# The experts' second product with tokens instead of features on PSUM's partitions

## The chip, the core and the metric

One core of a Trainium2 chip runs the program. The metric is device time in microseconds (us) of one execution. Engines are named as in the profile: PE is TensorE, PEld its weight loads, DVE is VectorE, ACT is ScalarE, POOL is GpSimd, SP is the queue that issues the DMAs.

## What is computed

Linear attention on 4 batches of 576 rows, then four experts whose outputs are added with a weight per token, then a gated dense layer. Only the experts are touched by the change:

```python
def _moe_ref(x, domain_probs, w1, w2):          # x: 2304 tokens x 512
    p = domain_probs / (domain_probs.sum(-1, keepdims=True) + 1e-09)
    out = np.zeros((N, D), dtype=np.float32)
    for e in range(E):                          # 4 experts, 1024 hidden features each
        h = np.maximum(x @ w1[e], 0.0)
        out += p[:, e:e + 1] * (h @ w2[e])
    return out
...
    x = _moe_ref(x=x, **moe_kwargs)
    return _moe2_ref(x=x, **moe2_kwargs)        # (silu(x @ wg) * (x @ wv)) @ wo, 1536 hidden
```

## The kernel before

The 2304 tokens are worked on in two halves of 1152. A half has two blocks of columns: X has 512 tokens, Y has 640. Hidden features are cut into units of 256: 16 expert units (kind "e", 4 per expert) and 6 gated units (kind "g") in each half, 44 units in all, numbered 0 to 43; a step is one unit on one block, so a half has 32 expert steps and 12 gated ones. Every large float32 product is three passes of float32r: an operand is split into a high part (a cast on ACT, `split`, line 98) and the rest (a subtraction on DVE or POOL, line 99).

In a step, `stage_h` makes the hidden features by seven products of half-sized operands (Winograd's form of Strassen's, `chain`). Each product is six matmuls on PE, of 256 columns for X and 320 for Y; their sums lie in three PSUM banks. ACT copies the first bank away after products 1, 6, 7 and 4 (`sn`, line 482, and line 500), and DVE adds (lines 488, 497, 503) to get four quadrants of `g`. In an expert step DVE then applies the ReLU and the token's weight in one instruction on each half of the tokens (`expert`, line 623), ACT casts the high part `hh` (line 628), and DVE makes the low part `hl` at the start of the next step (line 632). The weights lie on all 128 partitions in the order of the columns (`pbc`), brought there by broadcasting DMAs.

`stage_y` is the second product. In the step after, in chunks between the seven products, it multiplies `hh` and `hl` by the unit's second weights (`oh`, `ol`). In an expert step the weights are the stationary operand and the tokens move: a tile is 128 model features by 256 or 320 tokens, six matmuls long, and there are eight of them; DVE adds each to `acc` (line 701), which is kept transposed, features on partitions. In a gated step the tokens are stationary: a tile is 128 tokens by 512 features, and there are four (X) or five (Y); DVE adds with line 716.

`WEAVE` says after which of the step's products how many chunks of the step before run. PE and ACT execute from step 2 on in the order of the program; DVE and POOL in the order that a scheduler gives them when the kernel is built. Where an operand is not ready, the engine waits and so does all that stands behind it on that engine. PSUM's eight banks are held by tags with a number of buffers: `hA` and `hB` two each, `hC`, `at` one each, `y` two.

At the turn from experts to gated units (unit 15 to 16, and 37 to 38), the sums in `acc` become the next layer's tokens. `combine_x` makes seven operands of them, in two stages for each pair of model tiles (j = 0, 1): casts on ACT (`xh`), low parts on DVE and POOL (`xl`), four subtractions on DVE in place (lines 396 to 399), then more casts and low parts. Steps count from 0: in a half of 44 steps, ML = 32 is the step of the first gated unit on X, and `AX_`, `AY_` say at which product of ML-1 and ML each stage is issued.

While the first half's experts run, other work shares the engines: the attention of batches 2 and 3, and the decoding of the gated layers' float64 weights, 36 pieces with five DVE instructions each (lines 538 to 545). In the second half nothing of that is left.

## Time and profile before

| | |
|---|---|
| device time, median of 3 executions | 1384.72 us (1378.69 to 1385.62) |
| the profiled execution: span from first to last instruction | 1383.4 us |
| PE busy | 1289.2 us, 93% of the span |
| DVE busy | 1141.1 us, 82% |
| ACT busy, POOL busy | 595.6 us (43%), 569.7 us (41%) |
| mean granted TensorE clock | 0.976 of full |
| from the first product of unit 2 on X to that of unit 15 on Y (first half's experts) | 131.4 to 511.3 us |
| units 24 to 36 (second half's experts) | 821.5 to 1128.9 us |

The span of the profiled execution lies inside the range of the three times. Busy shares over the whole span are means over stages with different limits, so the stages are read one by one. PE's busy time overlaps itself, because matmuls are pipelined: the time that a matmul takes from the next one is the distance of their starts.

### The profile page before, as it was taken

What the parts mean: (1) busy time and instruction counts of PE and PEld (TensorE: products, weight loads), DVE (VectorE), ACT (ScalarE), POOL (GpSimd) and SP (SyncE); (2) the same over time, 40 slices, a digit from 0 to 9 for tenths busy, and PEclk for the clock granted to TensorE, in tenths of its full rate; (3) what the DMA queues carried; (4) which work ended last, traced back from release to release, by engine and by line L of the source; (5) the groups of instructions that cost most, each with busy time, mean ns of one, the idle gap of its engine ahead of it and who ended that gap; (6) DMA issues with size and microseconds to landing.
All of it is one profiled execution on the core that took longest, in us unless ns stands there. A gap on an engine that the chain in (4) does not pass through costs nothing.

```text
span 1383.4 us, 23002 instructions
## 1 busy us (share of the span) xinstructions
PE 1289.2 (93%) x8809; PEld 1224.2 (88%) x8809; DVE 1141.1 (82%) x2169; ACT 595.6 (43%) x1292; POOL 569.7 (41%) x547
## 2 busy tenths in 40 slices
PE   4688989999899997999999899999999999999998
PEld 3578988898888997889898799999999998899997
DVE  7887899999999989887878976666666679877775
ACT  3553334344344434654555533333333334544442
POOL 3453533344333627543333644343435355444420
PEclk9689999999999999999999999999999999999999
DMA  8310244445354421211112402111111111211101
GB/s 203 96 54 24 92 161 135 137 133 164 115 163 124 144 69 56 78 49 55 54 63 88 150 16 70 56 46 51 59 32 64 46 47 31 62 46 47 47 1 69
DMA packets 85794, 110.61 MB, mean 80 GB/s; under 512 B 28524, under 2 KB 55220, under 8 KB 85684
## 3 DMA queue, kind: packets, MB, share of 16 engines
q1 hardware_dynamic: 85684, 109.15, 26.0%
q8 instruction: 69, 1.13, 0.3%
q14 instruction: 41, 0.34, 0.1%
HBM read 92.57 MB, written 16.55 MB: 79 GB/s over the span
## 4 chain that ended last, share of the span: by engine, by line
PE 60%; DVE 30%; issue 3%; ACT 2%; POOL 2%; DMA 1%; SPq 0%; DVEq 0%; POOLq 0%; ACTq 0%
PE y L104 6%; PE y L103 6%; PE y L105 6%; PE h L103 5%; PE h L104 5%; PE h L105 5%; DVE acc L701 4%; DVE hl L632 3%; PE o L711 3%; PE o L709 3%; PE o L710 3%; DVE g L623 3%; DVE xl L99 2%; DVE r L543 2%; PE h_1g L103 1%
## 5 line engine op out<-in xcount | busy, mean ns | idle before, releaser
L104 PE MATMUL y<-hl,oh 128*128 128x320 f32 (+1 forms) x1024 | 305.1, 298 | 5.2 <-DVE hl L632 4.8
L103 PE MATMUL y<-hh,oh 128*128 128x320 f32 (+1 forms) x1024 | 305.8, 299 | 4.3 <-DVE acc L701 1.8
L105 PE MATMUL y<-hh,ol 128*128 128x320 f32 (+1 forms) x1024 | 303.8, 297 | 0.0
L701 DVE TENSOR_TENSOR acc<-y,acc 128x256 f32<-128x256 f32 (+1 forms) x480 | 207.4, 448 | 65.8 <-PE y L105 62.1
L104 PEld LDWEIGHTS y<-hl,oh 128*128 128x128 f32 x1024 | 195.6, 191 | 8.2 <-DVE hl L632 8.0
L628 ACT CAST hh<-g 128x512 fp32r<-128x512 f32 (+1 forms) x176 | 118.2, 675 | 195.1 <-DVE g L623 134.5
L103 PEld LDWEIGHTS y<-hh,oh 128*128 128x128 f32 x1024 | 195.9, 191 | 6.8 <-DVE acc L701 3.0
L105 PEld LDWEIGHTS y<-hh,ol 128*128 128x128 f32 x1024 | 195.8, 191 | 0.0
L482 ACT COPY sn<-h 128x256 f32<-128x256 f32 (+1 forms) x192 | 76.6, 399 | 214.9 <-PE h L105 212.9
L632 DVE TENSOR_TENSOR hl<-g,hh 128x512 fp32r<-128x512 f32 (+1 forms) x176 | 158.7, 906 | 5.2 <-ACT hh L628 4.8
L623 DVE SCALAR_TENSOR_TENSOR g<-g,pbc 128x512 f32<-128x512 f32 (+1 forms) x128 | 119.5, 934 | 27.7 <-ACT g L500 27.1
L709 PE MATMUL o<-oh,hh 128*128 128x512 f32 x216 | 86.4, 400 | 0.0
L711 PE MATMUL o<-oh,hl 128*128 128x512 f32 x216 | 85.6, 397 | 0.5 <-DVE hl L632 0.5
L710 PE MATMUL o<-ol,hh 128*128 128x512 f32 x216 | 85.7, 397 | 0.0
L716 DVE TENSOR_TENSOR acc<-o,acc 128x512 f32<-128x512 f32 x90 | 61.5, 684 | 25.7 <-PE o L711 24.3
L657 DVE TENSOR_TENSOR g<-g,s 128x256 f32<-128x256 f32 (+1 forms) x96 | 56.6, 616 | 24.3 <-ACT s L653 24.2
L500 ACT COPY g<-h 128x256 f32<-128x256 f32 (+1 forms) x64 | 25.6, 400 | 112.7 <-PE h L105 112.7
L99 POOL TENSOR_TENSOR xl<-acc,xh 128x256 fp32r<-128x256 f32 (+3 forms) x24 | 30.6, 1281 | 59.9 <-ACT xh L98 55.2
L711 PEld LDWEIGHTS o<-oh,hl 128*128 128x128 f32 x216 | 40.9, 189 | 11.4 <-DVE hl L632 1.9
L497 DVE TENSOR_TENSOR g<-h,sn 128x256 f32<-128x256 f32 (+1 forms) x64 | 28.9, 451 | 22.8 <-ACT sn L482 22.7
L653 ACT ACTIVATE s<-g 128x256 f32<-128x256 f32 (+1 forms) x96 | 39.4, 443 | 18.7 <-DVE g L503 17.4
L709 PEld LDWEIGHTS o<-oh,hh 128*128 128x128 f32 x216 | 41.0, 190 | 6.0 <-ACT hh L628 0.6
(1166 smaller groups left out, 4036.2 us busy)
## 6 DMA issues: line engine op xcount, KB each, us to landing
r<-in_moe_w_gate_dram SPq DMA_DIRECT2D x12, 512.0 KB, 3.8
r<-in_moe_w_val_dram SPq DMA_DIRECT2D x12, 512.0 KB, 4.0
r<-in_moe_w_out_dram SPq DMA_DIRECT2D x12, 512.0 KB, 4.3
out_dram<-acc SPq DMA_DIRECT2D x16, 256.0 KB, 2.4
w_g<-r SPq DMA_DIRECT2D x12, 256.0 KB, 2.4
...
```

Of the source, the lines that this page charges most:

```text
L103: nc.tensor.matmul(o, wh, xh, start=first, stop=False, skip_group_check=more)
L104: nc.tensor.matmul(o, wh, xl, start=False, stop=False, skip_group_check=more)
L105: nc.tensor.matmul(o, wl, xh, start=False, stop=last, skip_group_check=more)
L482: nc.scalar.copy(sn[z], banks[0])
L623: nc.vector.scalar_tensor_tensor(g[:, :, t], g[:, :, t], 0.0, pbc[hf, e, b][:, None, ts].to_broadcast([P, 2, n]), ALU.max, ALU.mult)
L628: nc.scalar.copy(hh[:, :, t * n:(t + 1) * n], g[:, :, t])
L632: (nc.vector, nc.vector)[t].tensor_tensor(hl[:, :, ts], g[:, :, t], f32(hh[:, :, ts]), ALU.subtract)
L701: nc.vector.tensor_tensor(y, p, y, ALU.add)
L709: nc.tensor.matmul(p, hh[:, z, ts], w[z][0], start=z == 0, stop=False)
L710: nc.tensor.matmul(p, hh[:, z, ts], w[z][1], start=False, stop=False)
L711: nc.tensor.matmul(p, hl[:, z, ts], w[z][0], start=False, stop=z == NF - 1)
L716: nc.vector.tensor_tensor(o, p, o, ALU.add)
```

## The change

The experts' second product now has the gated layers' form: tokens stationary, 512 features moving, so a tile is 128 tokens by 512 features and a block has four (X) or five (Y) of them. A token's weight is then one number per partition, and DVE applies it where it adds the tile to `acc`. The line `expert` goes; the ReLU moves into ACT's cast and into DVE's subtraction. `acc` now holds tokens on partitions, so at the turn PE transposes it back (`turn_x`, 128 by 128 each, 16 for X and 20 for Y in a half), ACT copies the result into SBUF (`turned_x`, tag `xt` with two buffers), and `combine_turned` works on the copies. For X the low parts at the turn all go to DVE (`LOWX`), for Y POOL keeps its share (`LOWY`). The DMAs of `pbc`, and the small transposition before them, go. Chunks are now half a tile (three matmuls), and `WEAVE` spreads them: two after each of products 5, 6, 7, 4 and 3.

The second product's tiles take turns over three banks (`TURNS`), and the second bank of a chain alternates between two from step to step.

```diff
-        def expert(t):
-            ts = slice(t * n, (t + 1) * n)
-            nc.vector.scalar_tensor_tensor(
-                g[:, :, t], g[:, :, t], 0.0, pbc[hf, e, b][:, None, ts].to_broadcast([P, 2, n]), ALU.max, ALU.mult
-            )
         def high(t):
-            nc.scalar.copy(hh[:, :, t * n:(t + 1) * n], g[:, :, t])
+            nc.scalar.activation(hh[:, :, t * n:(t + 1) * n], g[:, :, t], AF.Relu if kind == "e" else AF.Copy)
         def low(t):
             ts = slice(t * n, (t + 1) * n)
-            (nc.vector, nc.vector)[t].tensor_tensor(hl[:, :, ts], g[:, :, t], f32(hh[:, :, ts]), ALU.subtract)
+            if kind == "e":
+                nc.vector.scalar_tensor_tensor(hl[:, :, ts], g[:, :, t], 0.0, f32(hh[:, :, ts]), ALU.max, ALU.subtract)
+            else:
+                nc.vector.tensor_tensor(hl[:, :, ts], g[:, :, t], f32(hh[:, :, ts]), ALU.subtract)
...
+        for t in range(2 * n // P):
+            p = ps("Y" if kind == "e" and st % HL != ML and st > 1 else "y", f"o{i}_{b}_{t}")
+            ts = slice(t * P, (t + 1) * P)
+            for z in range(NF):
+                nc.tensor.matmul(p, hh[:, z, ts], w[z][0], start=z == 0, stop=False)
+                nc.tensor.matmul(p, hh[:, z, ts], w[z][1], start=False, stop=False)
+                nc.tensor.matmul(p, hl[:, z, ts], w[z][0], start=False, stop=z == NF - 1)
+                if z < NF - 1:
                     yield
+            o = accO[b][:, t, :]
+            if kind == "e":
+                weight = pn[:, hf * NTT + C0[b] // P + t, e:e + 1]
                 if first:
+                    nc.vector.tensor_scalar(o, p, weight, None, ALU.mult)
                 else:
+                    nc.vector.scalar_tensor_tensor(o, p, weight, o, ALU.mult, ALU.add)
...
+    def turn_x(b, z, tag):
+        nt = 2 * N[b] // P
+        for t0 in range(0, nt, 4):
+            n = min(4, nt - t0)
+            tp = ps(tag, f"xtp{b}{z}{t0}")
+            for t in range(n):
+                nc.tensor.transpose(tp[:, t * P:(t + 1) * P], accO[b][:, t0 + t, z * P:(z + 1) * P], ident)
+            turning.append((b, z, t0 * P, n * P, tp))
+
+    def turned_x(n):
+        for b, z, t0, nt, tp in turning[:n]:
+            if t0 == 0:
+                turned[b, z] = sbt("xt", [P, 2 * N[b]], f"xt{b}{z}")
+            nc.scalar.copy(turned[b, z][:, t0:t0 + nt], tp[:, :nt])
+        del turning[:n]
...
-        "turn0": [0, 2, 2, 1, 14, 1, 15, 9],
-        "turn1": [0, 0, 1, 4, 7, 0, 8, 13],
-        "e": [0, 0, 0, 2, 2, 0, 0, 5],
+        "turn": [0, 4, 4, 2],
+        "before": [0, 0, 2, 4, 2],
+        "e": [0, 0, 2, 2, 2, 2, 2],
...
-    AX_ = [[(0, 3), (4, 7)], [(2, 5), (2, 4)]]
-    AY_ = [[(4, 7), (5, 10)], [(5, 8), (7, 10)]]
+    TX = [[(2, 5), (2, 5), (2, 7), (1, 1)], [(1, 2), (1, 2), (1, 5), (1, 6)]]
+    TY = [[(0, 4), (0, 5), (0, 6), (0, 7)], [(0, 7), (0, 7), (0, 9), (0, 10)]]
+    LOWX, LOWY = nc.vector, nc.gpsimd
...
+                    turn, done, *sums = [(st - back, pos) for back, pos in when[j]]
+                    for z in (2 * j, 2 * j + 1):
+                        at(*turn, turn_x, b, z, "y")
+                        if z == 2 * j and b == Y:
+                            at(*turn, turned_x, 2)
+                    at(*done, turned_x, 2)
+                    for p in sums:
+                        at(*p, combine_turned, b, j, LOWX if b == X else LOWY)
```

In `TX` and `TY` a pair is (steps before ML, product of that step), for the transposes, their copies, and the two stages of `combine_turned`, for j = 0 and j = 1.

What this does to DVE's order is seen in an ordinary expert step, unit 26 on Y (`g26_1`, with `y26_0` the tiles of unit 26 on X that run in it). Before:

```order
L497 TENSOR_TENSOR g26_1_10052<-h26_11_10074,sn26_13_10117 128x320
L701 TENSOR_TENSOR acc0_68<-y26_0_0_1_10120,acc0_68 128x256
L701 TENSOR_TENSOR acc0_68<-y26_0_1_1_10128,acc0_68 128x256
L623 SCALAR_TENSOR_TENSOR g26_1_10052<-g26_1_10052,pbc1_1_1_10047 128x2x320
L503 TENSOR_TENSOR g26_1_10052<-h26_11_10074,sn26_12_10089 128x320
L701 TENSOR_TENSOR acc0_68<-y26_0_0_2_10154,acc0_68 128x256
L623 SCALAR_TENSOR_TENSOR g26_1_10052<-g26_1_10052,pbc1_1_1_10047 128x2x320
L701 TENSOR_TENSOR acc0_68<-y26_0_1_2_10162,acc0_68 128x256
L701 TENSOR_TENSOR acc0_68<-y26_0_0_3_10170,acc0_68 128x256
L632 TENSOR_TENSOR hl26_1_10054<-g26_1_10052,hh26_1_10053 128x2x320
L701 TENSOR_TENSOR acc0_68<-y26_0_1_3_10178,acc0_68 128x256
L632 TENSOR_TENSOR hl26_1_10054<-g26_1_10052,hh26_1_10053 128x2x320
```

The same step on DVE with the change, complete, from its first addition to its second low part (the tiles are now `o26_0_0` to `o26_0_3`):

```order
L503 TENSOR_TENSOR g26_1_8892<-h26_12_8905,sn26_11_8902 128x320
L715 SCALAR_TENSOR_TENSOR acc0_68<-o26_0_0_8923,pn_71,acc0_68 128x512
L715 SCALAR_TENSOR_TENSOR acc0_68<-o26_0_1_8943,pn_71,acc0_68 128x512
L512 TENSOR_TENSOR g26_1_8892<-h26_11_8914,sn26_13_8957 128x320
L715 SCALAR_TENSOR_TENSOR acc0_68<-o26_0_2_8960,pn_71,acc0_68 128x512
L642 SCALAR_TENSOR_TENSOR hl26_1_8894<-g26_1_8892,hh26_1_8893 128x2x320
L715 SCALAR_TENSOR_TENSOR acc0_68<-o26_0_3_8975,pn_71,acc0_68 128x512
L518 TENSOR_TENSOR g26_1_8892<-h26_11_8914,sn26_12_8937 128x320
L503 TENSOR_TENSOR g27_0_8995<-h27_02_9008,sn27_01_9005 128x256
L642 SCALAR_TENSOR_TENSOR hl26_1_8894<-g26_1_8892,hh26_1_8893 128x2x320
```

The two weightings of `g26_1` are gone, and four additions of 512 columns stand where eight of 256 were. Both low parts still close the step.

On PE, at the turn of the second half, step 37 on Y (ML-1): between product 5 (`h37_11`) and product 6 (`h37_10`) there stand now two groups of transposes of X's sums and the first tile of `o36_1`, where before product 6 followed product 5 at once. With the change:

```order
L112 MATMUL h37_11_11440<-xh1_817,wl37a_11081 128x320
L412 MATMUL xtp020_11449<-ident_66,acc0_68 128x128 x4
L412 MATMUL xtp030_11454<-ident_66,acc0_68 128x128 x4
L704 MATMUL o36_1_0_11463<-oh360_10991,hh36_1_11280 128x512
L705 MATMUL o36_1_0_11463<-ol360_10992,hh36_1_11280 128x512
L706 MATMUL o36_1_0_11463<-oh360_10991,hl36_1_11281 128x512
L704 MATMUL o36_1_0_11463<-oh361_11076,hh36_1_11280 128x512
L705 MATMUL o36_1_0_11463<-ol361_11077,hh36_1_11280 128x512
L706 MATMUL o36_1_0_11463<-oh361_11076,hl36_1_11281 128x512
L110 MATMUL h37_10_11417<-xh1_817,wh37a_11080 128x320
```

The two groups fill both buffers of tag `y`, and `o36_1_0` is given the buffer of the first of them, so it starts when ACT has copied `xtp020` out.

On ACT, in the step of the first gated unit on X (ML, unit 38 on X), with the change, from the copy after product P1v to the copy of the last transposes of Y:

```order
L497 COPY sn38_0v1_11662<-h38_0v0_11655 128x256
L419 COPY xt10_11671<-xtp100_11664 128x512
L419 COPY xt10_11671<-xtp104_11669 128x128
L419 COPY xt11_11689<-xtp110_11674 128x512
L419 COPY xt11_11689<-xtp114_11679 128x128
L497 COPY sn38_0g3_11698<-h38_0g0_11567 128x256
L105 CAST xh1_817<-xt10_11671 128x320
L105 CAST xh1_817<-xt11_11689 128x2x320
L105 CAST xh1_817<-xt10_11671 128x2x320
L105 CAST xh1_817<-xt11_11689 128x2x320
L419 COPY xt12_11729<-xtp120_11722 128x512
L419 COPY xt12_11729<-xtp124_11727 128x128
```

Before, the same stretch of ACT's order had no copies, and the casts read the sums themselves:

```order
L482 COPY sn38_0v1_13496<-h38_0v0_13489 128x256
L98 CAST xh1_825<-acc1_69 128x320
L98 CAST xh1_825<-acc1_69 128x2x320
L482 COPY sn38_0g3_13544<-h38_0g0_13401 128x256
L98 CAST xh1_825<-acc1_69 128x320
L98 CAST xh1_825<-acc1_69 128x2x320
L500 COPY g38_0_13397<-h38_0g0_13401 128x256
L98 CAST xh1_825<-acc1_69 128x2x320 x2
```

What moved: eight copies stand among the casts now. The copies `xt12` take the buffer of `xt10`, so ACT can make them only when every reader of `xt10` is done, POOL's low part among them; and the transposes of the next pair wait for those copies, because `y` has two banks.

## Rows read from the trace of the kernel before

**Rows 1.** The page's busy times, and DVE in 40 slices of the span
```profile
PE 1289.2 (93%) x8809; PEld 1224.2 (88%) x8809; DVE 1141.1 (82%) x2169; ACT 595.6 (43%) x1292; POOL 569.7 (41%) x547
...
DVE  7887899999999989887878976666666679877775
```

**Rows 2.** Windows: stretch, length; busy (records) of PE, PEld, DVE, ACT, POOL; clock, DMA
```profile
43.70:131.40 87.70, 71.70 (x424) 64.20 (x422) 74.25 (x174) 39.33 (x92) 41.07 (x45) 0.83 0.15 46
131.40:511.30 379.90, 350.74 (x2539) 340.86 (x2539) 363.03 (x710) 152.59 (x319) 150.91 (x134) 0.98 0.42 131
511.30:575.30 64.00, 54.89 (x345) 50.49 (x344) 59.82 (x104) 33.06 (x72) 40.23 (x38) 0.95 0.17 51
575.30:765.20 189.90, 186.28 (x1184) 170.78 (x1183) 155.09 (x285) 105.03 (x231) 74.11 (x74) 1.00 0.22 68
...
821.50:1128.90 307.40, 307.40 (x2341) 307.40 (x2341) 211.74 (x404) 114.03 (x236) 124.94 (x118) 1.00 0.17 53
1153.80:1196.20 42.40, 37.40 (x242) 33.78 (x241) 38.14 (x62) 21.38 (x48) 24.33 (x20) 1.00 0.13 38
1196.20:1353.40 157.20, 157.20 (x1005) 144.97 (x1004) 120.25 (x192) 72.71 (x170) 56.90 (x54) 1.00 0.13 38
```

**Rows 3.** Waits of PE, all stages: us in total, times, longest
```profile
PE h L103 <- DVE g L497: 24.8, 22, 2.5
```

**Rows 4.** Lines on DVE, first half's expert steps: busy us, mean ns, idle before
```profile
L701 DVE TENSOR_TENSOR acc<-y,acc 128x256 f32<-128x256 f32 (+1 forms) x215 | 90.8, 445 | 7.0 <-PE y L105 5.9
L623 DVE SCALAR_TENSOR_TENSOR g<-g,pbc 128x640 f32<-128x640 f32 (+1 forms) x56 | 51.7, 923 | 3.5 <-ACT g L500 3.4
```

**Rows 5.** Timeline of DVE, both halves: start, us, what
```profile
227.23 1.78 DVE L623 SCALAR_TENSOR_TENSOR g<-g,pbc 128x512 f32<-128x512 f32 x1
...
229.27 0.47 DVE L701 TENSOR_TENSOR acc<-y,acc 128x320 f32<-128x320 f32 x1
229.67 1.05 DVE L623 SCALAR_TENSOR_TENSOR g<-g,pbc 128x512 f32<-128x512 f32 x1
...
843.25 0.41 DVE L701 TENSOR_TENSOR acc<-y,acc 128x256 f32<-128x256 f32 x1
843.58 0.81 DVE L623 SCALAR_TENSOR_TENSOR g<-g,pbc 128x640 f32<-128x640 f32 x1
844.31 0.76 DVE L701 TENSOR_TENSOR acc<-y,acc 128x256 f32<-128x256 f32 x2
```

**Rows 6.** Lines by shape on DVE, whole span: the addition of 512 columns
```profile
L716 DVE TENSOR_TENSOR acc<-o,acc 128x512 f32<-128x512 f32 x90 | 61.5, 684 | 25.7 <-PE o L711 24.3
```

**Rows 7.** Timeline of PE: transposes; first and last of runs of 24, 24, 11
```profile
381.53 0.38 PE L319 MATMUL qtp<-ident,e 128*128 128x128 f32 x2
...
400.08 0.31 PE L103 MATMUL y<-hh,oh 128*128 128x320 f32 x1
...
403.43 0.31 PE L105 MATMUL y<-hh,ol 128*128 128x320 f32 x1
...
413.18 0.28 PE L103 MATMUL y<-hh,oh 128*128 128x256 f32 x1
...
415.89 0.28 PE L105 MATMUL y<-hh,ol 128*128 128x256 f32 x1
...
702.16 0.40 PE L709 MATMUL o<-oh,hh 128*128 128x512 f32 x1
...
704.47 0.40 PE L710 MATMUL o<-ol,hh 128*128 128x512 f32 x1
```

**Rows 8.** Timeline at the second turn: two casts on ACT, then POOL's low part
```profile
1171.27 1.36 ACT L98 CAST xh<-acc 128x640 fp32r<-128x640 f32 x2
...
1172.08 1.59 POOL L99 TENSOR_TENSOR xl<-acc,xh 128x640 fp32r<-128x640 f32 x1 [0.53 <-ACT xh L98]
```

**Rows 9.** Timeline of PE, a wait in brackets; window behind it, columns as above
```profile
239.93 0.41 PE L103 MATMUL h<-xh,wh5a 128*128 128x320 f32 x1 [1.86 <-ACT sn L482]
...
241.30:244.70 3.40, 3.02 (x12) 3.02 (x13) 3.36 (x8) 0.52 (x2) 0.12 (x1) 0.50 0.54 147
```

121 lines of the change are left out of this document (43 added, 78 removed), and 2 rows, old and new, of the table BUFS.

## The prediction, made before the changed kernel was run

> **What bounds the kernel now.** The page comes first: PE is busy 93% of the span and DVE 82%, and DVE's slices stand mostly at 8 or 9 through the first 23 of 40 and at 6 or 7 behind them [rows 1]. So I went to the windows by stage, because the two halves do the same expert work [rows 2]. In the second half 26 expert steps take 307.4 us, 11.82 each; PE is busy in all of it, DVE in 211.7 (69%). In the first half 27 such steps take 379.9 us, 14.07 each, with DVE busy for 363.0 (96%). The attention of the other batches accounts for little of that on PE: 2539 records against 27 x 90, that is 109 more, which at 0.11 us (an estimate: most are transposes, and two of those end in 0.38 [rows 7], 0.19 each at most; 256 columns take 0.118 by the pace worked out below, 128 half of it at least) are 12 us. PE's need there is 27 x 11.82 + 12 = 331 us, and 49 us are waiting. DVE is what it waits for: the longest entry among PE's waits is product 3 waiting for line 497, 24.8 us at 22 places [rows 3]. Second-half expert steps are bound by PE, first-half ones by DVE.
>
> **The change, part by part.** *Line 623 goes.* In the first half's stretch it is 56 instructions and 51.7 us of DVE [rows 4]. Undisturbed it is cheaper: from 843.58 to 844.31 is 0.73 us for 640 columns, so about 0.60 for 512 (an estimate at the same rate), 28 x 1.33 = 37 us. The rest is disturbance: the mean is 923 ns, and one of 512 columns took 1.78 [rows 4, 5]. Line 701, which reads PSUM, shows no such spread (mean 445 over both shapes; 0.40 from start to start for 320, 0.33 for 256 [rows 5]). I take 52, and 37 as the bound if other instructions inherit the disturbance. The Trainium skill (SBUF — State Buffer, SBUF: two separate sides) says that a DVE instruction with two SBUF inputs and a GpSimd one that reads SBUF lock each other out for a whole instruction. These rows fit it. By it the lock is lost with line 623 only if no other two-input instruction is next in POOL's way, and hl, the decoding and the low parts are such; so it speaks for the 37, the row for the 52.
>
> *The additions* become fewer and longer: for X 8 x 0.33 = 2.64 against 4 of 512 columns. One of those takes 0.684 [rows 6], less the 0.08 by which neighbours overlap (0.41 against 0.33 [rows 5]), 0.60; 2.40. For Y 8 x 0.40 = 3.20 against 5 x 0.60 = 3.00. Over 27 steps that is 6 us. The weight rides in the same instruction; line 623, also a two-operation form, runs one column per cycle like a plain addition, so I add nothing. ReLU in the cast and the subtraction costs nothing for the same reason. DVE's need falls from 363 to about 305.
>
> *PE's tiles.* From start to start a matmul takes (403.43 - 400.08)/23 = 0.146 us at 320 columns, (415.89 - 413.18)/23 = 0.118 at 256, (704.47 - 702.16)/10 = 0.231 at 512 [rows 7]. The columns are the same: 48 x 0.146 becomes 30 x 0.231 (7.01 to 6.93), 48 x 0.118 becomes 24 x 0.231 (5.66 to 5.54). That is 0.2 us for a unit: 2.5 in each half's stretch. Halving the weight loads gives no more, since they lie under the matmuls.
>
> *First half's expert steps.* PE needs 331 - 2 = 329, DVE 305: the order of the two turns round. Some waiting stays, since both are above 85%. The nearest stretch with a similar pair is the gated steps of the first half: ten steps, DVE 155.1 of 189.9 (82%). At the second half's 157.2/9 each, plus 67 attention records of 0.11, they would take 182; they lose 4%. I take 4%, 13 us: 342 instead of 380, **-38**. Bounds: -51 with no waiting left; -26 if the 24.8 us at line 497, which come in bursts, all stay.
>
> *Start and second half's start.* Before 131.4 DVE is busy 74.3 of 87.7 us [rows 2] and holds 7 of line 623 (the steps that begin there, counted in the program), at 0.92 each 6 us [rows 4]; part of that is waited for elsewhere: **-4** (0 to -8). The first four expert steps of the second half hold 6 to 7 of them while the loaded columns are combined on DVE: **-3** (0 to -5).
>
> *Second half's expert steps* are PE's: **-2**. That needs the new additions to hide. A tile takes PE 6 x 0.231 = 1.39 us, DVE 0.60, and three banks take turns, so a bank has 2.8 us to be emptied. The first tile now comes after product 5, one product sooner, and needs the first low part. From the end of product 4 that leaves at least product 3 and products 1, 2, 5 of the next step (4 x 0.7) and a tile, 4.2 us; the chain is copy, cast, subtraction, some 2.4 us with hand-offs. Covered, while DVE's queue is short.
>
> *The turn* is where work is added. 36 transposes in a half, 0.11 each: 4 us of PE. Then the waits, in PE's order. X, j = 1: tile o36_1_0 stands behind two groups of transposes and gets the first group's bank, so it waits for ACT's copy of it; that copy stands behind casts that wait for DVE's four subtractions, and its buffer of `xt` is that of j = 0, whose low part DVE must have finished. From the end of product 3 DVE has to do lines 518 and 503 (0.8), two low parts of hl (1.5), two low parts (0.9), three subtractions (1.0), then a cast 0.6, a low part 0.6 and a copy 0.6: 6.0, with seven hand-offs of 0.13 (a cast of 0.68 begun at 1171.27, POOL at 1172.08 [rows 8]) 6.9. PE has 18 x 0.146 and eight transposes, 3.5. Wait 3.5; another 1.5 in step ML, where the first low part of hl stands behind j = 1's sums on DVE. Y, j = 0 to 1: ACT's copies `xt12` need POOL's low part of `xt10`. Behind product 7: a copy and a cast (0.8), cast 0.68, DVE 0.73, three subtractions of 0.40, cast 0.68, POOL 1.59 [rows 8], copies 0.7, with hand-offs 7.2; PE has one product and five transposes, 1.3. The second group waits about 5.5. The two banks of `y` cost 1 before that. Behind it j = 1's two stages follow with one product between (9 and 10), so product 7 and 4 of the gated chain wait for copies that stand behind casts: 3. Sum 4 + 3.5 + 1.5 + 5.5 + 1 + 3 = 18.5. What this replaces: the second turn's 42.4 us hold 84 x 0.118 + 48 x 0.146 and 84 x 0.146 + 24 x 0.231 = 34.7 of PE, 7.7 lost; the first turn's 64.0 hold those and an expert step of 13.2 and some attention, about 49, 15 lost [rows 2]. Second turn +11; first, where DVE is full and six of line 623 go, I take 20 instead of 15, **+5**. Bounds +2 and +36 for both.
>
> Sum: -38 - 4 - 3 - 2 + 11 + 5 = -31. The profiled span is 1383.4, 1.3 under the median of the runs, so **1352**.
>
> **Rivals.** *The turn is cheap*: DVE and POOL catch up as they do now, and of the waits only the transposes come on top. +2 instead of +16: 1338. For it: six fewer line 623. Against it: the buffers above. Chance 0.2. *DVE stays the bound*: the disturbance moves to other instructions, DVE keeps 320 of the new span. At 93% it would lose as now, half of the 49 us, and the burst bound holds: -26 or worse with the rest unchanged, and a dearer turn beside it, 1364 to 1372. Chance 0.16. The lock rule above gives this case. *The clock falls at the turn*: after PE waited 1.86 us up to 239.93, the granted clock stood at 0.50 from 241.3 to 244.7, the lower level, 1.2 GHz [rows 9]; 1.7 us lost each time. Four such at each turn would cost 14 us more in all, and 2 more for the queues that they find full: 1368. Chance 0.1. The Trainium skill (TensorE: Matmul & The Clock Gate, Part 4: PE-mode transpose) says that transposes don't count as busy for the gate, which would favour this; the two here are too few to show it. *On the other side*: the second low part stands late in DVE's order while the first tile comes a product sooner. If the tile waits in each of the 62 steps, it decides at 0.5 us a step; at 0.8 the time is 1402. For it: DVE works in order and the first half's queue is long. Against it: the 1.8 us of slack, and DVE at 57% in the second half (211.7 less 26 x 1.33, of 307.4). Chance 0.05.
>
> **How the numbers follow.** The forecast has 0.49. The range 1332 to 1376 takes in the cheap turn with a better first half and the two dear cases. What a measurement here can tell from no change is about 0.5%, 7 us. All of the first three rivals are faster except their upper edges: faster 0.86, same 0.08, slower 0.06.
>
> **What would show it.** Expert steps of the first half at 12.5 to 12.9 us with DVE near 89%; second-half steps at 11.7 to 11.9 with PE still full; the additions of 512 columns at 0.68; two waits of PE of over 3 us in each turn, released by ACT's copies of the transposes; the turn's stretches longer than now. Wrong would be: additions slowed beyond 0.7, second-half steps with gaps before the new tiles, or a turn shorter than before.

## The result, and the profile after

The changed kernel takes 1397.42 us (median of 4 executions, 1396.40 to 1398.93), the kernel before 1383.99 (4 executions on the same chip); the ratio is 1.0105 with a 95% interval of 1.0083 to 1.0126. It is 1% slower, where 1352 was forecast. The profiled execution has a span of 1395.1 us, 11.7 more than before.

The page's busy times and slices of the changed kernel show DVE's relief:

```profile
PE 1292.2 (93%) x7536; PEld 1150.2 (82%) x7536; DVE 1044.9 (75%) x1824; ACT 604.6 (43%) x1316; POOL 538.6 (39%) x539
...
DVE  7885979889899786797888856555555556877775
...
PEclk9689999999999998999999999999999998999999
```

DVE's busy time fell by 96 us, PE's stayed within 3. The windows by stage, with the same borders as [rows 2] moved to the new times, show where the time went (columns as there):

```profile
127.60:494.30 366.70, 343.35 (x1978) 300.84 (x1976) 321.07 (x555) 151.87 (x320) 139.97 (x134) 0.99 0.42 130
494.30:572.30 78.00, 61.39 (x336) 53.59 (x336) 59.44 (x103) 37.81 (x84) 34.02 (x34) 0.89 0.13 38
...
762.20:818.50 56.30, 51.06 (x278) 44.88 (x277) 41.36 (x59) 22.14 (x45) 26.25 (x23) 0.94 0.28 90
818.50:1124.30 305.80, 305.80 (x1795) 274.65 (x1794) 176.84 (x261) 113.69 (x237) 119.80 (x118) 1.00 0.15 47
1124.30:1208.30 84.00, 70.72 (x398) 63.22 (x397) 55.31 (x91) 38.45 (x85) 30.87 (x29) 0.92 0.09 26
```

| stage, from the first product of ... | before | after | change | forecast |
|---|---|---|---|---|
| start, to unit 2 on X | 131.4 | 127.6 | -3.8 | -4 |
| first half's experts, to unit 15 on Y | 379.9 | 366.7 | -13.2 | -38 |
| first turn, to unit 17 on X | 64.0 | 78.0 | +14.0 | +5 |
| second half's start, units 22 and 23 | 56.3 | 56.3 | 0 | -3 |
| second half's experts, to unit 36 on Y | 307.4 | 305.8 | -1.6 | -2 |
| second turn, to unit 39 on X | 67.3 | 84.0 | +16.7 | +11 |

The stages of gated units stayed within 0.4 us. Two rows carry the difference: the first half's experts lack 25 us, the turns have 15 too many.

In the first half's experts DVE is busy for 321 us of 366.7, 42 less than before. PE's need was forecast at 329 us, so by that need 38 are still lost, where 49 were. The waits in that stretch (engine, what waits, what it waits for; us, times, longest), PE's longest before the change and then those with it:

```profile
PE h L103 <- DVE g L497: 23.1, 20, 2.5
```

```profile
PE h L110 <- DVE g L512: 14.9, 11, 2.6
...
DVE r L553 <- DMA r<-in_moe_w_gate_dram: 8.5, 7, 2.5
DVE r L553 <- DMA r<-in_moe_w_out_dram: 8.1, 6, 1.7
...
DVE r L553 <- DMA r<-in_moe_w_val_dram: 5.9, 5, 2.4
```

PE waits for the same addition of the chain as before (line 497 then, 512 now), 14.9 us in place of 23.1, and DVE, which had hardly waited for the loads of the float64 pieces (1.2 us before), now waits 22.5 us for them. DVE's lines there:

```profile
L715 DVE SCALAR_TENSOR_TENSOR acc<-o,pn,acc 128x512 f32<-128x512 f32 x121 | 89.7, 742 | 13.4 <-PE o L706 13.1
L642 DVE SCALAR_TENSOR_TENSOR hl<-g,hh 128x512 fp32r<-128x512 f32 (+1 forms) x55 | 45.1, 820 | 1.1 <-ACT hh L637 0.9
...
L558 DVE SCALAR_TENSOR_TENSOR r<-r 128x512 int32<-128x512 int32 x36 | 31.1, 863 | 0.6
...
L557 DVE TENSOR_SCALAR r<-r 128x512 int32<-128x512 int32 x36 | 21.4, 593 | 0.5
```

The addition of 512 columns takes 742 ns where 684 had been read from the gated one [rows 6]; over 121 of them that is 7 us. The decoding is where it was: 863 and 593 ns, before the change 855 and 600:

```profile
L543 DVE SCALAR_TENSOR_TENSOR r<-r 128x512 int32<-128x512 int32 x36 | 30.8, 855 | 0.2
...
L542 DVE TENSOR_SCALAR r<-r 128x512 int32<-128x512 int32 x36 | 21.6, 600 | 0.2
```

What makes it long is seen in DVE's timeline beside that of POOL:

```profile
273.17 0.74 DVE L715 SCALAR_TENSOR_TENSOR acc<-o,pn,acc 128x512 f32<-128x512 f32 x1
273.84 1.53 DVE L553 TENSOR_SCALAR r<-r 128x512 int32<-128x512 int32 x1
275.29 0.41 DVE L512 TENSOR_TENSOR g<-h,sn 128x256 f32<-128x256 f32 x1
275.62 1.17 DVE L555 TENSOR_SCALAR r<-r 128x512 f32<-128x512 f32 x1
...
272.78 1.06 POOL L474 TENSOR_TENSOR raw8a<-raw8a 128x256 f32<-128x256 f32 x1
273.80 2.70 POOL L106 TENSOR_TENSOR wl8a<-raw8a,wh8a 128x512 fp32r<-128x512 f32 x2
```

Line 553 works on 512 int32 columns; its median in this stretch is 0.43 us, and it takes 1.53 here, while POOL makes a low part of the weights. POOL's pair of 2.70 us is one instruction up to 275.08 and one up to 276.50; line 553 ends at 275.37 and line 555, which takes 1.17, at 276.79, each 0.29 us after the instruction on POOL. The additions at 273.17 and 275.29, which read PSUM, are as short as ever. So what [rows 4, 5] showed on line 623 holds the decoding too, and there the change has not taken it away.

At the second turn, the waits of PE from 1124.3 to 1208.3, the two longest in PE's timeline, and what ACT does ahead of them:

```profile
PE xtp L412 <- ACT xt L419: 5.9, 2, 5.3
PE o L704 <- ACT xt L419: 4.2, 1, 4.2
PE o L706 <- DVE hl L642: 2.1, 1, 2.1
```

```profile
1144.79 0.54 PE L704 MATMUL o<-oh,hh 128*128 128x512 f32 x1 [4.17 <-ACT xt L419]
...
1181.29 1.33 PE L412 MATMUL xtp<-ident,acc 128*128 128x128 f32 x5 [5.30 <-ACT xt L419]
...
1142.72 1.14 ACT L105 CAST xh<-xt 128x512 fp32r<-128x512 f32 x2 [2.49 <-DVE xt L386]
1144.15 1.19 ACT L419 COPY xt<-xtp 128x512 f32<-128x512 f32 x2 [0.29 <-DVE xl L106]
...
1180.65 0.75 ACT L419 COPY xt<-xtp 128x512 f32<-128x512 f32 x2 [1.02 <-POOL xl L106]
```

Both waits stand where they were forecast. The copy that gives `o36_1_0` its bank begins at 1144.15, behind casts that waited 2.49 us for DVE's subtractions; the copy `xt12` begins at 1180.65, when POOL's low part is done. What the sum did not hold is the clock behind the waits:

```profile
1145.20:1148.40 3.20, 3.20 (x11) 2.71 (x10) 0.75 (x1) 0.14 (x1) 0.00 (x0) 0.50 0.00 0
1162.20:1165.40 3.20, 3.20 (x12) 2.61 (x11) 3.20 (x5) 0.00 (x0) 3.04 (x3) 0.50 0.00 0
1179.20:1186.00 6.80, 4.71 (x22) 4.71 (x23) 2.92 (x4) 3.93 (x10) 2.30 (x2) 0.50 0.00 0
```

Three stretches of the second turn, 3.4, 3.4 and 7.1 us long by finer windows, at the lower level of 1.2 GHz: two behind the waits of 4.2 and 2.1 us, the third from within the wait of 5.3 us on. In the kernel before the turn's clock stood at 1.00 [rows 2].

### The profile page after: what moved, and what is told of

It is laid out like the page before. It is cut to its first block, busy times and chain, and to the rows that moved or that the text cites. A ratio compares the mean times of both kernels' runs of the same rounds, so it can differ in the third digit from the quotient of the medians.

```text
span 1395.1 us, 20129 instructions
## 1 busy us (share of the span) xinstructions
PE 1292.2 (93%) x7536; PEld 1150.2 (82%) x7536; DVE 1044.9 (75%) x1824; ACT 604.6 (43%) x1316; POOL 538.6 (39%) x539
## 4 chain that ended last, share of the span: by engine, by line
PE 63%; DVE 22%; DMA 6%; issue 4%; ACT 3%; POOL 1%; SPq 0%; DVEq 0%; POOLq 0%; ACTq 0%
PE o L706 9%; PE o L704 9%; PE o L705 9%; PE h L110 6%; PE h L111 5%; PE h L112 5%; DVE acc L715 3%; DMA r<-in_moe_w_out_dram 2%; DMA r<-in_moe_w_gate_dram 2%; DVE hl L642 2%; DVE r L560 1%; PE h_1g L111 1%; PE h_1g L110 1%; PE h_1g L112 1%; PE h_1v L111 1%
## 5 line engine op out<-in xcount | busy, mean ns | idle before, releaser
L704 PE MATMUL o<-oh,hh 128*128 128x512 f32 x792 | 318.3, 402 | 14.0 <-ACT xt L419 9.4
L706 PE MATMUL o<-oh,hl 128*128 128x512 f32 x792 | 316.2, 400 | 7.4 <-DVE hl L642 7.0
L705 PE MATMUL o<-ol,hh 128*128 128x512 f32 x792 | 315.9, 399 | 0.0
L715 DVE SCALAR_TENSOR_TENSOR acc<-o,pn,acc 128x512 f32<-128x512 f32 x270 | 201.2, 746 | 132.4 <-PE o L706 132.1
L706 PEld LDWEIGHTS o<-oh,hl 128*128 128x128 f32 x792 | 151.0, 191 | 46.8 <-DVE hl L642 9.7
L704 PEld LDWEIGHTS o<-oh,hh 128*128 128x128 f32 x792 | 150.9, 190 | 34.9 <-ACT xt L419 9.9
L637 ACT ACTIVATE hh<-g 128x512 fp32r<-128x512 f32 (+1 forms) x176 | 120.4, 686 | 122.2 <-DVE g L518 65.3
L705 PEld LDWEIGHTS o<-ol,hh 128*128 128x128 f32 x792 | 150.9, 190 | 19.9 <-DVE ol L106 0.6
L642 DVE SCALAR_TENSOR_TENSOR hl<-g,hh 128x512 fp32r<-128x512 f32 (+1 forms) x128 | 115.0, 907 | 20.4 <-ACT hh L637 20.0
L644 DVE TENSOR_TENSOR hl<-g,hh 128x512 fp32r<-128x512 f32 (+1 forms) x48 | 53.5, 1114 | 2.9 <-ACT hh L637 2.3
L663 ACT ACTIVATE s<-g 128x256 f32<-128x256 f32 (+1 forms) x96 | 39.4, 442 | 16.3 <-DVE g L518 16.2
L512 DVE TENSOR_TENSOR g<-h,sn 128x256 f32<-128x256 f32 (+1 forms) x64 | 28.9, 452 | 16.4 <-ACT sn L497 16.4
```

The source lines that it names most:

```text
L637: nc.scalar.activation(hh[:, :, t * n:(t + 1) * n], g[:, :, t], AF.Relu if kind == "e" else AF.Copy)
L642: nc.vector.scalar_tensor_tensor(hl[:, :, ts], g[:, :, t], 0.0, f32(hh[:, :, ts]), ALU.max, ALU.subtract)
L704: nc.tensor.matmul(p, hh[:, z, ts], w[z][0], start=z == 0, stop=False)
L705: nc.tensor.matmul(p, hh[:, z, ts], w[z][1], start=False, stop=False)
L706: nc.tensor.matmul(p, hl[:, z, ts], w[z][0], start=False, stop=z == NF - 1)
L715: nc.vector.scalar_tensor_tensor(o, p, weight, o, ALU.mult, ALU.add)
```

## The experiments

Stretch means below the first half's expert steps (unit 2 on X to unit 15 on Y), turn the second one, read from the profile of each run with the borders of the table above. A stretch is of one execution: in the changed kernel and the four runs that edit only its turns it is 366.7, 367.6, 370.6, 370.6 and 367.0, so differences under 4 us in it tell nothing. Ratios are to the kernel before on the same chip; the changed kernel's is 1.0105.

| run | median us | ratio (95%) | stretch | turn |
|---|---|---|---|---|
| e1_no_loads | 1391.25 | 1.0038 (1.0023 to 1.0053) | 361.1 | 83.7 |
| e2_before_no_loads | 1390.19 | 1.0025 (1.0009 to 1.0041) | 385.6 | 67.4 |
| e3_no_transposes | 1379.26 | 0.9957 (0.9940 to 0.9974) | 367.6 | 72.1 |
| e4_early_loads | 1402.98 | 1.0120 (1.0104 to 1.0135) | 369.9 | 84.0 |
| e5_before_no_weighting | 1375.04 | 0.9936 (0.9912 to 0.9960) | 373.7 | 65.4 |
| e6_little_pool | 1373.95 | 0.9925 (0.9905 to 0.9946) | 344.2 | 84.0 |
| e7_kv_copies | 1396.90 | 1.0089 (1.0067 to 1.0111) | 370.6 | 81.8 |
| e8_warm | 1396.46 | 1.0088 (1.0066 to 1.0111) | 370.6 | 80.4 |
| e9_apart | 1405.55 | 1.0148 (1.0126 to 1.0169) | 373.7 | 84.0 |
| e10_before_little_pool | 1344.24 | 0.9707 (0.9683 to 0.9731) | 340.3 | 68.3 |
| e11_before_apart | 1391.04 | 1.0047 (1.0031 to 1.0063) | 388.0 | 68.3 |
| e12_scratch_pool | 1450.69 | 1.0461 (1.0438 to 1.0484) | 345.5 | 83.9 |
| e13_short_pool | 1391.21 | 1.0040 (1.0028 to 1.0053) | 361.6 | 84.0 |
| e14_before_short_pool | 1372.48 | 0.9904 (0.9888 to 0.9920) | 369.4 | 67.1 |
| e15_third_bank | 1391.57 | 1.0045 (1.0028 to 1.0063) | 367.0 | 77.3 |
| e16_scratch_beside | 1394.46 | 1.0053 (1.0038 to 1.0068) | 364.0 | 83.8 |
| e17_before_shorter_pool | 1379.26 | 0.9947 (0.9915 to 0.9979) | 374.2 | 66.4 |
| e18_after_both | 1385.96 | 0.9995 (0.9984 to 1.0006) | 362.7 | 77.4 |

**Are the loads what DVE loses by (e1, e2)?**

```diff
-        nc.sync.dma_start(
+        if n < 2: nc.sync.dma_start(
```

> The changed kernel, with the loads of the float64 pieces left out from the third piece on (their decoding works on old data). In the changed kernel DVE waits 22.5 us for these loads in the first half's expert steps (18 waits at line 553, up to 2.5 us), before the change 1.2 us. Theory A, the loads: additions of the chain stand behind these waits in DVE's order, and most of the 33 us that PE loses there comes from them. Then this stretch (127.6 to 494.3, 366.7 us) takes 345 to 352 and the whole 1375 to 1384. Theory B, the amount of DVE work: at 88% busy DVE can't follow PE closely, and the waits lie where it had nothing to do anyway. Then the stretch stays within 5 us of 366.7 and the whole at 1391 or above.

> The kernel before, with the same loads left out. Theory A and theory B: DVE hardly waited for loads here (1.2 us), so 1378 to 1386, no change. A third theory, C: the loads disturb DVE or the other DMAs by their traffic; then both kernels gain alike, and this one falls by 8 us or more, below 1376.

The changed kernel as a whole fell by 0.7%, its stretch by 5.6 us, where theory A wanted 15 or more; the kernel before rose by 0.25%, its stretch by 5.7. In e1 DVE still waits 11.6 us at line 553, now for the stores of earlier pieces, so the edit took away about half of the wait. So far the loads look like a small part (e6 below bears this out); theory A in its strong form is out, and so is C, a gain in both.

**Loads earlier, by closer decoding (e4).**

```diff
-            at((z + (0, 2, 4)[x]) // 8, (z + (0, 2, 4)[x]) % 8, stage[x], n)
+            at((z + (0, 1, 2)[x]) // 8, (z + (0, 1, 2)[x]) % 8, stage[x], n)
-                at((z + 7) // 8, (z + 7) % 8, decode_load, n + 2)
+                at((z + 4) // 8, (z + 4) % 8, decode_load, n + 2)
```

> The changed kernel with a piece's three groups of decoding at positions 0, 1, 2 (0, 2, 4 before) and its successor's load at 4 (7 before), so that between a load and the first instruction on it lie 6.4 positions of a step instead of 3.4. Theory A: DVE's waits for loads fall from 22.5 to under 8 us and the stretch of the first half's experts by 8 to 18, the whole to 1379 to 1389. Theory B: the decoding comes denser, PE waits more for the chain's additions, and the whole is 1397 or more.

The stretch is not shorter, and DVE's waits for loads are 24.9 us: DVE reached the line earlier too, so the edit did not take the wait away. The time is theory B's, but its mechanism is not seen: PE waits 14.5 us for line 512, no longer than without the edit.

**Line 623 out of the kernel before, alone (e5).**

```diff
         def expert(t):
             ts = slice(t * n, (t + 1) * n)
-            nc.vector.scalar_tensor_tensor(
-                g[:, :, t], g[:, :, t], 0.0, pbc[hf, e, b][:, None, ts].to_broadcast([P, 2, n]), ALU.max, ALU.mult
-            )
+            pass
```

> The kernel before with line 623 left out (no ReLU and no weight), all else as it was: the removal alone. Without the loads the changed kernel's first-half stretch fell only by 5.6 us, so theory A is down to that share. Theory B, DVE is still what bounds: the other disturbed instructions take the disturbance over, a smaller DVE load shortens the stretch by about a third to a half of what is taken away; then the stretch of the first half's experts (379.9) takes 360 to 370 here too, and the whole 1364 to 1375 (its turns stay at 64 and 67). Theory D, the new form costs there by itself (an addition of 0.74 us stands ahead of the chain's additions in DVE's order, where before one of 0.42 to 0.48 stood): then the removal alone gives 345 to 355, the whole 1345 to 1358.

The whole lies at the upper edge of theory B's range, the stretch above it. The window of the stretch, and PE's wait in it:

```profile
129.80:503.50 373.70, 347.06 (x2540) 340.05 (x2539) 325.53 (x655) 151.07 (x319) 141.87 (x134) 0.98 0.42 128
...
PE h L103 <- DVE g L497: 22.1, 12, 3.3
```

DVE's busy time fell by 37 us of the 51.7 that line 623 had held, and the stretch by 6.2. PE waits 22.1 us for line 497 as before (23.1 in this stretch). Taking the instruction away buys 6 us. D, a price of the new form, is not needed to explain why the change gained only 13 there, and B's price (a third to a half of the load) was too high as well. What makes the changed kernel's stretch another 7 us shorter than this one is not shown; 2.5 of it was reckoned for PE's tiles.

**Little work on POOL (e6, e10).** ACT copies in place of POOL's low parts, from unit 3 to 15; in the sums only 16 of 128 columns.

```diff
+        few = 16 if nm[:-1].isdigit() and 3 <= int(nm[:-1]) < 16 else P
+        def part(h, l, src):
+            nc.scalar.copy(h, src)
+            if few < P:
+                nc.scalar.copy(l, src)
+            else:
+                low.tensor_tensor(l, src, f32(h), ALU.subtract)
...
-        split(hi[:, 0:2], lo[:, 0:2], rv[:, :, :, 0:P], low)
+        part(hi[:, 0:2], lo[:, 0:2], rv[:, :, :, 0:P])
```

> The changed kernel with little work on POOL in the first half's experts: from unit 3 on ACT copies the weights in place of POOL's low parts, and POOL's sums of weights take 16 columns of 128; values are others. By the trace DVE's instructions took 65 us longer in that stretch than the shortest tenth of their kind, before the change (66) and after it (65), though line 623 is gone. Theory B1: this excess comes from POOL's instructions beside them, and keeps DVE the bound. Then the excess falls below 25 us, DVE's busy time from 321 to about 275, and the stretch from 366.7 to 340 to 350, the whole to 1372 to 1383. Theory B2: the excess has another cause (or PE's waits come from the order alone): the stretch stays above 360 and the whole above 1390.

> The kernel before with the same cut of POOL's work in the first half's experts. If theory B1 holds for both kernels, line 623 (923 ns) and the decoding come down to their undisturbed times, DVE's busy time in the stretch from 363 to about 310 to 320, and the stretch from 379.9 to 350 to 360; the whole to 1355 to 1366, still below the changed kernel with the same cut (1374) since the turns differ by 31. If POOL's effect is one of the new form alone, the stretch stays above 370.

The window of e6's stretch with three lines of its decoding (the fourth, first and third instruction; last in a line is the idle time before it and what ended it), then the window of e10's and its weighting:

```profile
126.60:470.80 344.20, 337.48 (x1978) 298.53 (x1976) 279.65 (x555) 181.09 (x385) 24.33 (x69) 1.00 0.45 139
...
L570 DVE SCALAR_TENSOR_TENSOR r<-r 128x512 int32<-128x512 int32 x36 | 26.3, 732 | 0.6
...
L565 DVE TENSOR_SCALAR r<-r 128x512 int32<-128x512 int32 x36 | 16.3, 454 | 30.1 <-DMA r<-in_moe_w_val_dram 11.6 <-DMA r<-in_moe_w_out_dram 10.4 <-DMA r<-in_moe_w_gate_dram 8.1
L569 DVE TENSOR_SCALAR r<-r 128x512 int32<-128x512 int32 x36 | 15.3, 425 | 0.5
```

```profile
131.80:472.10 340.30, 337.28 (x2540) 332.14 (x2539) 312.82 (x710) 181.90 (x384) 29.65 (x69) 1.00 0.47 147
...
L639 DVE SCALAR_TENSOR_TENSOR g<-g,pbc 128x640 f32<-128x640 f32 (+1 forms) x56 | 42.2, 754 | 4.7 <-ACT g L512 4.5
```

POOL's busy time falls from 140 to 24 us, DVE's by 41, and PE, at 1.00 of its clock, waits 6.6 us in all, where it waited 23.3: the stretch takes 344.2, as B1 had it. DVE waits 30.1 us for the loads here, more than in the changed kernel, so these waits by themselves cost PE little. In the kernel before the same cut gives 340.3, less than the changed kernel's, though line 623 is still there: at 754 ns in place of 923 it costs PE next to nothing (waits of 2.7 us in all). That was more than expected (350 to 360). So with POOL quiet the first half is bound by PE in both forms, and what the change takes off DVE is worth nothing there.

**Decoding apart from POOL's weights (e9, e11).**

```diff
-            z = 50 + n * 52 // 10
+            z = 48 + n // 3 * 16 + (7, 10, 15)[n % 3]
...
-                at((z + 7) // 8, (z + 7) % 8, decode_load, n + 2)
+                at((z + 4) // 8, (z + 4) % 8, decode_load, n + 2)
```

> The changed kernel with the decoding kept apart from POOL's weights, nothing left out: POOL prepares weights at positions 2 to 7 of the steps on X, so the pieces start at position 7 of a step on X and at 2 and 7 of the step on Y behind it, three for a pair of steps, as many as before; a load goes out when its buffer's decoding ends. With little POOL work the stretch fell from 366.7 to 344.2, with the loads gone only to 361.1. Theory B1 (what holds the first half is that POOL's and DVE's instructions slow each other): the int32 lines of the decoding, 593 to 863 ns now, come down to 430 to 720, and the stretch falls to 348 to 358, the whole to 1380 to 1390. Theory B3 (it was the amount of work on POOL or the date of the weights, not what runs beside it): the stretch stays within 4 us of 366.7 and the whole above 1393.

> The kernel before with the decoding at the same places as in the kernel with decoding apart. Line 623 keeps its own disturbance where it falls beside POOL's weights, so the gain should be smaller than the changed kernel's: theory B1 says 4 to 12 us less than 379.9 in the stretch and 1372 to 1381 for the whole. Theory B3: no change, within 3 us.

Both were slower. In e9 DVE waited 35.6 us at line 553 for the stores of the pieces before (16.2, 12.8 and 6.6 for the three kinds of weights), a wait that the edit made by placing the pieces close together. In e11 these waits are 9.5 us, and DVE is busy for 365 us, 2 more than without the edit, so the pieces did not get out of POOL's way. B1's expectation failed in both; with new waits in the one and DVE's time as it was in the other, they tell nothing on B1 and B3.

**POOL busy on something else (e12, e16).** e6 with subtractions on POOL into a tile that nobody else uses; in e16 each reads the high part that ACT has just cast:

```diff
+    def beside(n, x):
+        s = scratch.rearrange("p (s n) -> p s n", s=2)
+        for z in range(n):
+            nc.gpsimd.tensor_tensor(s, s, x, ALU.subtract)
...
             if few < P:
                 nc.scalar.copy(l, src)
+                beside(2, f32(h)[:, 0:2] if len(h.shape) == 3 else f32(h)[:, 0])
```

> The changed kernel with little POOL work on weights (ACT copies them, values are others), and at the same places of the program subtractions on POOL of a tile of 256 columns that nobody else reads or writes, two for each low part and four for the sums, about as much POOL time as was taken out. The cut alone brought the stretch of the first half's experts from 366.7 to 344.2 and DVE's busy time from 321 to 280. Theory B1 (contention): POOL's instructions slow DVE's whatever they work on; then DVE's int32 lines are at 590 to 860 ns again, its busy time at 310 or more, and the stretch at 358 or more, the whole at 1388 or more. Theory B3 (dates): what counted was that the weights' low parts, and the buffers behind them, came earlier; then the stretch stays at 342 to 350, the whole at 1372 to 1380.

> Again the changed kernel with the cut of POOL's work and subtractions of 256 columns on POOL into a tile nobody reads, but now each reads the high part that ACT has just cast, so that they run where POOL's low parts ran, and not all at the start, as they did. Theory B1 (contention): DVE's int32 lines are slow again (the third and fourth of the decoding above 0.55 and 0.8 us), its busy time is at 305 or more, and the stretch at 354 or more, where the cut alone gave 344.2; the whole is at 1384 or more. Theory B3 (the dates of the weights and of their buffers): the stretch stays at 342 to 350, the whole at 1372 to 1380.

In e12 the subtractions waited for nothing, so POOL ran most of them at the start (unit 2 began at 201.8 us in place of 127.6): inconclusive. In e16, the window of the stretch and three lines of DVE:

```profile
127.60:491.60 364.00, 343.96 (x1977) 300.19 (x1975) 310.89 (x555) 182.12 (x385) 183.55 (x251) 0.99 0.43 131
...
L743 DVE SCALAR_TENSOR_TENSOR acc<-o,pn,acc 128x512 f32<-128x512 f32 x121 | 89.6, 743 | 14.7 <-PE o L734 14.5
...
L581 DVE SCALAR_TENSOR_TENSOR r<-r 128x512 int32<-128x512 int32 x36 | 29.6, 823 | 0.6
...
L580 DVE TENSOR_SCALAR r<-r 128x512 int32<-128x512 int32 x36 | 18.3, 510 | 0.5
```

The stretch is back at 364.0 and DVE at 311, with subtractions that nobody waits for; POOL is busy for 184 us here, more than the 140 of the changed kernel, so the run shows the effect and not its exact size. The addition of 512 columns, which reads PSUM, stays at 743 ns. B1 holds: POOL's instructions lengthen DVE's also where they write a tile that nobody uses, and PE's waits come back with them (19.9 us in all, 8.7 of them for the chain's addition). The third instruction of the decoding, at 510 ns, stayed below the 0.55 us expected, the fourth is at 823. For the dates of the weights (B3) nothing is left that could be told from no difference.

**Shorter instructions on POOL (e13, e14, e17).** The low parts in pieces of 256 columns, in e17 of 128:

```diff
+            if low is nc.gpsimd and not nm.startswith(("0", "1a", "2a")):
+                nc.scalar.copy(h, src)
+                for z in range(2):
+                    low.tensor_tensor(l[:, z], src[:, z], f32(h)[:, z], ALU.subtract)
```

> The changed kernel, nothing left out, with POOL's low parts of the weights in pieces of 256 columns in place of 512. Theory B1: an instruction of DVE that meets one of POOL is held for as long as that one lasts, so half as long an instruction holds DVE less long; POOL's time grows by a fifth, and the stretch falls by 5 to 15, the whole to 1384 to 1394. Rival B4: DVE is held as long in sum, by twice as many: within 3 us of the changed kernel.

> The kernel before with the same shorter pieces on POOL. Theory B1: with line 623 there to be held as well, it gains no less than the changed kernel: the stretch from 379.9 to 362 to 374, the whole 1366 to 1380, which would beat both kernels. Rival B4: within 3 us of 1385.

> The kernel before with POOL's low parts of the weights in pieces of 128 columns; pieces of 256 gave 1372.5, with the stretch of the first half's experts at 369.4 in place of 379.9 and the third instruction of the decoding at 558 to 611 ns in place of 556 to 696. Theory B1: a shorter hold again, the stretch at 360 to 367, the whole at 1361 to 1370. Rival: POOL's own time grows too far (each piece has a fixed part) and the weights come late: 1372 or more.

The windows of the stretch in e14 and e17:

```profile
130.30:499.70 369.40, 344.38 (x2540) 334.60 (x2539) 350.57 (x710) 151.88 (x319) 171.53 (x186) 1.00 0.44 135
...
130.50:504.70 374.20, 348.87 (x2540) 339.30 (x2539) 339.27 (x710) 151.99 (x319) 206.03 (x290) 0.98 0.42 133
```

The kernel before gains 1% and 10.5 us in the stretch, though POOL's busy time rises from 151 to 172: e14 beats both kernels and leaves nothing out. The changed kernel gains 0.65%, from 1.0105 to 1.0040. With pieces of 128 the time is the rival's: POOL is busy 206 us, and the ratio is 0.9947, with an interval that just touches that of e14. The rival's reason is not seen: PE shows no wait for POOL's weights in the stretch, and DVE is busy for 339 us, less than in e14. Why the shorter hold gains less there stays open.

**The turn (e3, e7, e8, e15).** e3 reads the sums as they lie, without `turn_x` and the copies:

```diff
     def turn_x(b, z, tag):
-        nt = 2 * N[b] // P
...
-                nc.tensor.transpose(tp[:, t * P:(t + 1) * P], accO[b][:, t0 + t, z * P:(z + 1) * P], ident)
+        turned[b, z] = acc[b][:, z * 2 * N[b]:(z + 1) * 2 * N[b]]
```

> The changed kernel without the transposes and their copies at the turns: the operands are made from the sums as they lie, so their values are others. The turns (494.3 to 572.3 and 1124.3 to 1208.3) take 78.0 and 84.0 us; before they were 64.0 and 67.3. If the 30.7 us come from the transposes, the waits for their copies and the lower clock behind these waits, the whole falls by 24 to 34 us, to 1363 to 1373, and the granted clock of the second turn is 1.00 again. Rival: the new tiles and DVE's order at the turn cost by themselves (first tiles waiting for low parts, 2 us each turn, and what follows); then it falls by less than 18, to 1379 or above.

Its windows of the two turns:

```profile
495.30:565.80 70.50, 58.05 (x308) 50.61 (x308) 59.16 (x102) 33.63 (x74) 35.46 (x34) 0.90 0.14 42
1116.80:1188.90 72.10, 64.14 (x362) 56.87 (x361) 56.82 (x91) 32.92 (x73) 32.02 (x29) 0.95 0.10 30
```

The whole fell by 1.5%, some 20 us, between the two expectations, and the second turn's clock is 0.95 and not 1.00. Of the 30.7 us the transposes with their copies and what follows from them make 19.4 (78.0 to 70.5 and 84.0 to 72.1). 11.3 are left of the rival's kind: the first new tile waits 2.3 and 2.1 us for its low part there, as in the changed kernel, and the clock falls behind such waits too.

> The changed kernel where, at the second turn alone, the copies of Y's last two transposed tiles have buffers of their own (tag kv, idle there), so they don't wait for readers of the first two. Theory F: the wait of 5.3 us before the second group of Y's transposes is for this buffer (POOL's low part reads it); it falls below 2 us, one of three falls of the clock goes too, and the second turn (84.0) takes 77 to 80, the whole 4 to 7 less: 1391 to 1396 beside a changed kernel at 1399. Theory G: the copies stand behind casts in ACT's order, which wait for DVE's subtractions; the wait stays above 4 and the time within 2 us.

```diff
-                turned[b, z] = sbt("xt", [P, 2 * N[b]], f"xt{b}{z}")
+                copies[0] += 1
+                more = b == Y and z >= 2 and copies[0] > 2 * KD
+                turned[b, z] = sbt("kv" if more else "xt", [P, 2 * N[b]], f"xt{b}{z}")
```

The wait fell from 5.3 to 4.2 us, the turn by 2.2: mostly G. Behind POOL's low part stood ACT's own order, with the casts that wait for DVE.

> The changed kernel with matmuls of no use, 256 columns each, ahead of the three long waits of the second turn (28, 14 and 36, by 0.118 us: 3.3, 1.7 and 4.2 us, as long as the waits or a little shorter). If the clock falls because PE stood still, it stays at 1.00 in the second turn, the waits themselves hardly change, and the turn falls from 84.0 to 79 to 81, by 1.7 us for each of the three falls less what the matmuls add. If the clock falls for another reason, or the added matmuls delay what PE would do, the turn takes 84 or more.

```diff
+        at(HL + ML, 7, dummies, 36)
...
+        at(HL + ML - 1, 2, dummies, 28)
+        at(HL + ML, 1, dummies, 14)
```

The window of its second turn:

```profile
1126.40:1206.80 80.40, 75.36 (x477) 68.03 (x476) 55.61 (x91) 38.32 (x85) 30.94 (x29) 1.00 0.09 27
```

The clock stays at 1.00, and the turn is 3.6 us shorter although PE does 78 matmuls more: what the falls had cost beyond the waits themselves is returned by keeping PE at work. The whole shows only part of it (ratio 1.0088), as its first half happened to be longer.

> The changed kernel with, at the second turn alone, a third bank (tag at, idle there) for X's second transposes of each pair, so that the first tile of unit 36 on Y gets its bank without waiting for ACT's copy, and with the two further buffers for Y's copies, which alone brought the turn from 84.0 to 81.8. Theory H: the wait of 4.2 us goes, and with it one fall of the clock; the turn takes 74 to 77, the whole 6 to 9 less than the changed kernel. Rival I: the wait only moves, to the first product of the gated unit, since the chain of casts, subtractions and low parts behind the copies is as long; then the turn stays at 80 or more.

```diff
-                        at(*turn, turn_x, b, z, "y")
+                        at(*turn, turn_x, b, z, "at" if hf and b == X and z % 2 else "y")
```

The window of its second turn, and the wait of PE that is left there:

```profile
1124.40:1201.70 77.30, 67.26 (x398) 59.92 (x397) 54.88 (x91) 38.23 (x85) 30.79 (x29) 0.98 0.09 28
...
PE xtp L412 <- ACT xt L421: 4.8, 2, 4.2
```

The wait of 4.2 us at `o36_1_0` is gone, the clock stands at 0.98, the turn at 77.3, just above theory H's range and well below I's: the bank set most of that wait, not the chain behind it. A new wait of 1.7 us, for ACT's copy of a product, stands in the turn now.

> The changed kernel with what helped it: pieces of 256 columns on POOL (stretch 366.7 to 361.6) and the third bank and further buffers at the second turn (84.0 to 77.3). If both add up: 1381 to 1386, level with the kernel before. If the shorter pieces lengthen the start and the turns again (they did by 1 to 2 us each): 1386 to 1392.

With shorter pieces and the third bank the changed kernel is level with the kernel before (0.9995), as the first case said.

## Why the prediction was wrong

- **The step that failed** is the first half's expert steps: "PE needs 331 - 2 = 329, DVE 305: the order of the two turns round", with -38 behind it and -26 as the bound. Its ground was the sentence that DVE, 96% busy, is what PE waits for, read as 363 us of work. Part of this was not work but time for which POOL held DVE's instructions: summed over DVE's instructions in the stretch, what each took beyond the shortest tenth of its line and shape in that run is 61 us before, 50 in the changed kernel, 7 in e6 and 40 in e16. (The 66 and 65 in the expectation of e6 do not come out of the traces in this way.) Of the 61, line 623 had 10, and the other 50 stayed. e5 prices the removal alone at 6 us, e6 and e10 price POOL's work at 22 and 40. How a held instruction of DVE becomes a wait of PE is only in part seen: POOL makes weights for up to 10 us at a time, once in a pair of steps, but of PE's 23 us of waits 11 come 20 to 24 us after such a time begins, when it is over. That DVE's backlog carries them there is argued, not shown.
- **PE's need** was also too low. e6 and e10, less their waits of 6.6 and 2.7 us, leave 337.6 us each, so the 329 lacked some 8 (an estimate), and of the 38 us lost by it about 29 are a loss. The forecast of 342 is about what the stretch takes with POOL quiet.
- **The rival that came**, at a chance of 0.16, is "DVE stays the bound": DVE keeps 321 us where it said 320, for nearly the reason that it gave: the disturbance did not move to other instructions but stayed on them. Its -26 was too much, as was the bound that it used, which counted PE's waits at one line alone on a need of 329.
- **The removal's size**: the bound of 37 for line 623 "if other instructions inherit the disturbance" had the right size, 37 us in e5, though its reason holds in part alone: the excess of the other instructions rose there by 3 us. The additions gained nothing on DVE: 742 ns with the weight in them, not 684, and beyond the 0.7 us that the prediction named as a sign of being wrong. So DVE fell by 42, not 58. The rule that the prediction cited against the row was right: the Trainium skill (SBUF — State Buffer, SBUF: two separate sides) says that a DVE instruction in one of its 2-port modes, or with two SBUF inputs beside a GpSimd one that reads SBUF, and a GpSimd instruction exclude each other for a whole instruction. The rows agree: line 553, with one tensor read but 512 columns in 0.43 us, took 1.53 beside POOL and ended just after POOL's instruction, the additions that read PSUM kept their time, and e16 shows it with a tile that nobody else uses. Which of the rule's two conditions holds a line, no run here separates.
- **The loads** were not in the prediction at all. Relieved of line 623, DVE reaches the decoding before its load has landed and waits, 24.6 us in e5 and 22.5 in the changed kernel. What this costs is small: e1 puts it at some 0.7% of the whole, of which the stretch shows 5.6 us, and in e6 DVE waits 30.1 us for the loads while PE hardly waits.
- **The turns**: the mechanism was right, and the waits were sized nearly right for the second: 4.2 for 3.5, 2.1 for 1.5, 5.3 and 0.6 for 5.5 (7.2 less 1.3 is rather 5.9) and 1, but 0.9 in place of 3 behind them. The term that was missing is the clock, which stood among the rivals ("the clock falls at the turn", 0.1): up to 6.7 us of 84.0 by its mean of 0.92, and 3.6 by e8. For the first turn +5 was too low by 9: its waits are 16.4 us where 8.9 were, of which I had expected DVE's relief to take most, and its clock is 0.89 where it was 0.95.
- **Second half's start**: 0 and not -3. DVE's busy time fell there from 48.8 to 41.4 us, but PE's waits did not fall: 5.3 us in all, 4.9 before, now for POOL's low part (1.6 us), ACT's copy (1.5), a low part of `hl` (1.3) and a cast. e5 gained 1.8.
- **Right**: the start, -3.8 for -4, and the second half's experts, -1.6 for -2, with PE full and the first tile a product sooner; the rival of a wait in each of the 62 steps did not come.
- **The last sum** gave the span and not the time: 1383.4 less 31 is 1352, and the median of the runs lies 1.3 above the span.

What stays open: why the kernel before loses 40 us by POOL's work and the changed one only 22 (both end near PE's need), how much of the 22 needs POOL's holds and the waits for loads together, since both end in the same waits at line 512, and how the first turn's 14 us divide, which no run but e3 edited.
